# Gated linear attention and a PReLU MLP on one core: v's rows for all six levels through one copy in DRAM

## The chip, the cores and the metric

One core of a Trainium2 chip runs the whole kernel. The metric is device microseconds for one execution. The core has five engines with an instruction queue each: PE (matrix products), DVE (vector), ACT (scalar functions), POOL, and SP, which here issues all loads and stores. The data of a load or store is moved by 16 DMA engines that SP's queue feeds.

## The reference

```python
def _attn_ref(q, k, v, a_re, a_im):            # each (4, 8, 768, 48)
    mag = np.sqrt(a_re * a_re + a_im * a_im)
    scale = np.minimum(mag, 0.999) / (mag + 1e-06)
    a_re_n, a_im_n = (a_re * scale, a_im * scale)
    for t in range(S):
        ar, ai = (a_re_n[:, :, t, :, None], a_im_n[:, :, t, :, None])
        new_re = ar * S_re - ai * S_im
        new_im = ar * S_im + ai * S_re
        kv = np.einsum('bhd,bhe->bhde', k[:, :, t], v[:, :, t])
        S_re, S_im = (new_re + kv, new_im)
        y[:, :, t] = np.einsum('bhd,bhde->bhe', q[:, :, t], S_re)

def _moe_ref(x, w_in, w_out, alpha):           # x (3072, 384), d_ff 2048
    h = x @ w_in
    g = np.maximum(h, 0.0) + alpha * np.minimum(h, 0.0)
    return (g @ w_out).astype(np.float32)
```

The attention's y, with the heads of a token side by side, is the MLP's x. All is float32.

## The kernel before

**Tiling.** The sequence of each of the 4 batches is cut into 6 chunks of 128 tokens. A chunk of all 8 heads is a *unit* (24 units, u = 6 x batch + chunk). Two units make a *group* of 256 tokens, of which the MLP has 12.

**A unit.** Inside a chunk the recurrence is taken apart into six *levels*, h = 1, 2, 4, 8, 16, 32. At level h the chunk is cut into blocks of 2h tokens, and the queries of each block's second half meet the keys of its first half. DVE turns keys and queries by the phases (L579, L581) and multiplies them by decays step by step (L637, six times a unit). PE makes the products of each level (`ps_lv`, L596), DVE or ACT mask them into the tiles A, and PE multiplies A with the values of the blocks' first halves and adds all up in `ps_y` (L760). The state carried from chunk to chunk enters by L746. ACT copies the result out of PSUM (L771) and SP stores it as `ysc` (L776). `xT` (L792 and L797) is the same data read back as the MLP's input.

**The tile that the change is about.** `VL` holds for each level the values v that L760 needs: of each block of 2h tokens only h, those of its first half, shifted by one token since a unit's keys run from token 1 of the chunk. It has 128 partitions, of which each half of 64 serves two pairs of heads. One row of 96 numbers (384 bytes) is one token of two heads. There is one VL buffer, so it is loaded anew for each unit after the unit before has used it.

**How VL is filled.** Two tasks do it. `half_rows` (L480) copies, once a batch and for the levels 4, 8 and 16 only, the wanted tokens of all six chunks from v to a tensor `vsc` that also lies in DRAM: six transfers of 288 KB a batch, one for each level and each half of the heads. `loads_v` (L523 to L551) then fills VL for each unit: the levels 1, 2 and 32 directly from v (L547, ten transfers a unit), the levels 4, 8 and 16 from `vsc` (L551, two transfers). Before them it loads `V` (L523, L525, L528), all tokens of the chunk, for the state.

**The other loads.** `gates` turns the gate inputs into phases and decays, in nine pieces, and sends them to DRAM (`phs` L324, `decs` L361). `loads` brings per unit `KQ` (keys and queries, L499 and L501), `PP` (phases, L507) and `T` (decays, L514). `pieces` loads the MLP's weights in 16 pieces (L419), which ACT and DVE then put together into `w_in_sb` and `w_out_sb` (L435 to L445).

**The MLP.** The first two groups go feature by feature (`ps_h` L817, then ACT L824 and DVE L826, then `ps_o` L867). The other ten go two features at a time (L839, ACT L848 and L852, DVE L854) and through a scheme of seven half products (L957). PE takes 11,728 matmul instructions in all.

**What sets the order.** Every task is a generator; each letter of the string ORDER lets one of them go on by one step, and what that step emits is queued on its engine. So ORDER fixes, for each engine, the sequence of its instructions, SP's DMA issues included: A to I are the gate pieces, J is `loads`, K `half_rows`, L `loads_v`, M `pieces`, N and O the two weight matrices, P to m the units, n `loads_x`, o the MLP. Each engine works through its own sequence in order and waits where an input is not there yet. The numbers in `yield DMA(98)` and the like are costs by which such an order was laid out; they emit nothing.

Of the kernel before, what the change touches and what calls it, by code (L numbers as in the profile page):

```python
# [9 lines left out]
F32 = mybir.dt.float32  # L10
# [9 lines left out]
P = 128  # L20
# [7 lines left out]


ORDER = (  # L30
    "ABMAAAAMJBBABAAAAAAABAAAABAAAAAAMBBBMJJJMAAAABBAAAAAAAAAAAABBBAALKKLLJBBBBBBBBBPPPAKMNNNBJJMJBBBBBKB"
    "BPBBPBBBBBOPOPPPBPBBNJLJLBJJCCJJPPPPPNPPOOOPPLMJLLLLLKKPPQQCLLPONNNNNOOPOCCPCPPPPPPOQCNQPQPQPPCNNNCQ"
    "CCPMLLQQCCQPCCPNOOOCCCCQPPMMJJJMPPPQPQQNPPPPJLLLCQQLLJJLnJJCCNCCCCNNQQQRROQQCJLLLMJCLLLCQCCCQRNOCCCC"
    "CLLLQOQRRooooNQCCooQooQRQoOQoCRCoooooOQROQRNNQoRONoooQoooooROOMDNQQooRoOOoQQQQRQROQQRLJQLLQLDLLJJnLL"
    "LMLLLJNRDRoRRoooNDDNNSSRDRRRoRDooooRRRooRDoNoooRoRSoSRSDRoDRooooDSSoODoSoDoSSRRDRRLLLJMMJRooSRRooooR"
    "NRRLLRRLJJJLDDoSooNoNoooSoooJJMSNoooooSSDoSooooooOOONSooSSoooSSSSoToTTOSSooSJLJLJSSoooooooSooDTTDONN"
    "SSoooKLLKLLLLLLLTooSTToDNSTSTooooooooDDSOTSODOSSSSSSTTDTooTODTooooooooJMDoTNNoooooTLSSDTDTJJOTooOooo"
    "KnLLJLLJJoTOOOTTTDLLLULKLJLoToooTTooToDToUUoooooUTUToTTTooKJooooDDDDDoDoTUUoooooooDDDoooooooDLLLLDUU"
    "UUVoooooooVTTUTUTTTTVDTTLEULoooUUooooooUJJooooUUoJLEUEVUUUUUUEoooooooEooooUoUVoooEoooooUVEVVUoUUVUUo"
    "VVVEoUooVEEoKKLLLLLLLLLLLoJJJVUVUUUJoooUUooVooVoWVooooooooooEEUUEoVWEoooVVooVVVoVVoooooVVoVLLLJJLWoo"  # L40
    "oVWVVWWVEEoEWEEVVEVWWWWEVEEVLnLLLKLLLLLLooLJJJJoooooooVWVWVVVJWoVLVVooWEEoXWWoooooooooVLLEJJLLLLLJLL"
    "JJoEEEEoooooooEooLLLJLoWWWoWWLEooooooooWoXWoWoXooWoooWoooWooooEEoWooooWXXWooooWWEEEEEEooooooooooWXWW"
    "XWWWWWoJXXXoooWWoooooYoXoooooEXXoooooXXoooXLWWFLLLnJJJJFXoooooooFoJLLLLLLLLLJLLooooXXooYXFoXoXoXXXoo"
    "oooooYoXoooooXooooooXooooooXXYooYFFYXXYXYJYXYooFXFZFoYooooooooXXXXYXXoooLLLLooooYoYoYFFXXXXooYYooooo"
    "oooooooooZYYYYFooooYFFFFFooYYYooYoooYoooooJJLKKLLLJJJLLLLLLLJoooYYoooYFZZYZZFFYYJFZZFFaYYooooooooooY"
    "oooYYYYYooZFYFFLLFFoooooooooYLYLYLLZZoaoooooooooooFFnoooZZJJFZZFFFFooooZooZoFooooooooooFFoooooZooooo"
    "oooZZZZZZFFFoooLLJJLLLJLLLLFaZZoooooooZoKooZooooaZZaaZoZZaaaaZoooooooZZoZZZoaaoZaZaaooaJJGZLZGZGGZab"
    "JoooooooooooooboaaGoGGLJooGooooooooooooGaGGJLLbLLJLLLLLLLaaaaoooooaaooooooooooooooLKoGGaoaooooGbbGoo"
    "oooaaoooobbbJJKKaJooabbaooooGGGbGbGGcbGGaooooooooooooaabaaaaaabbbbaLLLLnJGGJLJooooooooooooooLLJJbcoo"
    "oooooooobbbbooooooooooooooooLKLGGGLLLbbbooooobbbbGccoooooooooooooocooobocGcLLLKKGbbbGcbbbcbooccooooo"  # L50
    "ooooooobbbbbccbbcGoooooGJJcccooooooooooooooGcccdoccoooocccoocccoLbLbLLLGGdLoGoooooJLJccoooocGcLJJJJL"
    "ccoGddoJLLeecLLLLGcooooooooooooodccdcccdooooodoccccdHddLLLJJonLoooooodddLLLLLHoHddooodHoooooooooJeHH"
    "oJLLLLLLJHoooooooooooooooeddeedddddoodoodeHoeodooodoooddooHoododdooooeeoHHoddoooddddeddeHdHHoooooooo"
    "oodoooooeooeHeeooeooLJLLLddLJLLJJJLLLJoooooooooooeeoooeHeeHeeeeeooooHHffeooooooooooooooeoJeoffJLLLLL"
    "efefeffefooffoeHoHeeeeooooefeooooooooooofeeoHHHJLeeJHfHnHooooooooooooooJoooLLJLLLLHHgffofooooHHgLJLL"
    "JHoooooooooofffoLJoJLLLLHHooooofoooHffoooooooooHgHffoooooooffgoooooHHHHHfooofofggfgffgggoooogohfooff"
    "fffffggogooooooooooogooooooffffIIIogghhJJKIooooooooooooLLLLLoooooggohgggooIIgogggoooogoooooooooogoog"
    "oooIhhgJJJJIoooooooooghgghgghohooooIhhooooooooooooooooIILJLLLLLLLLhghgghgIiihhIggIIhooooooohIIoooogg"
    "ILLLnJLLJooooooooooooooohhhhhhoIIIhhihoooooooohhooooooohohIooooooihiiiooooooooooiiohhhhoILLLLioooooo"
    "oooiIIooooooooohhLLLLiJJJJJLLhhhihhhoiLLLhhJJLLiiIIooioJJLLLLLLoooooooooooooiiooiiioooiiiijIIJJLLojI"  # L60
    "ooooioiooooooooiooiooIIiiiiijjooIJLoooooooooooooooooLijjiIIIjjjojojIIIoooooooooooooooooooIIjiiiijjij"
    "jioooooiLLLiLLLLnJLLoooooooooooooJJJJJLLLLLLjjjojjoojjojjjkoooooojjoooooooooojoooooooojjjjjjjooooooo"
    "kkkooojooooooooooooojkjkjJkoooookkkkooooooooooooooojkkooojjkkoLooooooookklooooooooooLLLLLLjjLLLkkkkk"
    "kkkkLLJJLLLJJJoooookooooookokookkooookkklooklloooooooookllkkolllokkooloooooolkoooollkklkkLJLLnlllooo"
    "ooooooooooooolllloooolllooolllooolooooooooooooooJJJoolooLLLmmLLLLLLLLLlomoomooooooloollllooooooooooo"
    "mlollmlllmLlllLLLLLLLLlmmooLLLLLmooooooooooomoooommooommmooooooooooooooooommmmmommomommooooomoooooom"
    "omoomooommmmmmmmmmmmmnoooooooooooooooooooooooooooooooooooooooooooooooooooooooooooooooooooooooooooooo"
    "oooooooooooooooooooooooooooooooooooooooooooooooooooooooooooooooooooooooooooooooooooooooooooooooooooo"
    "oooooooooooooooooooooooooooooooooooooooooooooooooooooooooooooooooooooooooooooooooooooooooooooooo")


class Ring:
# [25 lines left out]
def kernel(  # L98
# [32 lines left out]
    nc = tc.nc  # L131
# [6 lines left out]
    D2 = 2 * D  # L138
    HC = P // 2
# [6 lines left out]
    LEVELS = [h for visit in VISITS for h in visit]  # L146
# [5 lines left out]
    work = ctx.enter_context(tc.tile_pool(name="work", bufs=2))  # L152
# [33 lines left out]
    for h in (16, 32):  # L186
        by_row[h] = []
        for m in range(HC // h):
            t = next(column)
# [327 lines left out]
    def loads_v():  # L517
        for u in range(NU):
            b, c = divmod(u, NCH)
            yield DMA(172, ("KQ", u), takes=(R["V"],))  # L520
            L = loaded[u]
            L["V"] = V = work.tile([P, HP, D2], F32, tag="V", name="V", bufs=1)
            nc.sync.dma_start(V[0:P - 16], v[b, :, 1:P - 15, c].rearrange("n p e -> p n e"))  # L523
            t_ = yield DMA(24)
            nc.sync.dma_start(V[P - 16:P - 1], v[b, :, P - 15:P, c].rearrange("n p e -> p n e"))  # L525
            if c + 1 < NCH:
                t_ = yield DMA(2)
                nc.sync.dma_start(V[P - 1:P], v[b, :, 0:1, c + 1].rearrange("n p e -> p n e"))  # L528
            done["values", u] = t_
            yield DMA(98)  # L530
            VL = work.tile([P, len(LEVELS), 2, D2], F32, tag="VL", name="VL", bufs=1)
            first = True
            for k, h in enumerate(LEVELS):
                for i in range(2):
                    tokens = v[b, 2 * i:2 * i + 2, :, c].rearrange("n t e -> t n e")
                    to = VL[HC * i:HC * (i + 1), k]
                    if h <= 2:
                        runs = [(to[j::h], tokens[j + 1::2 * h]) for j in range(h)]
                    elif h == 32:
                        runs = [(to[h * m:h * (m + 1)], tokens[2 * h * m + 1:2 * h * m + h + 1]) for m in range(2)]  # L540
                    else:
                        runs = []
                    for dst, src in runs:
                        if not first:
                            yield DMA(98 // len(runs))
                        first = False
                        nc.sync.dma_start(dst, src)  # L547
            k = LEVELS.index(SPREAD[0])
            for i in range(2):
                t = yield DMA(49 * len(SPREAD), ("halves", u))  # L550
                nc.sync.dma_start(VL[HC * i:HC * (i + 1), k:k + len(SPREAD)].rearrange("p l n e -> p (l n) e"),  # L551
                                  vsc_of[u][i].rearrange("l n t e -> t (l n) e"))
# [351 lines left out]
    for m, f, c, n in blocks:  # L904
        if m < FIRST:
            i = place[m, f, c][0]
# [236 lines left out]
```

## Time and profile before

| what | us |
|---|---|
| median of three runs (766.57 to 769.87) | 768.29 |
| the profiled execution | 770.17 |
| its span, first to last instruction | 768.1 |
| PE busy | 676.6 |
| DVE busy | 605.7 |
| ACT busy | 489.4 |
| POOL busy | 12.3 |

The span is the core's own; the 2.1 us more of the profiled execution lie around it. The granted clock of PE was 0.993 on average. DMA moved 130.61 MB, at 170 GB/s on average; SP issued 700 transfers, of which 288 fill VL (240 directly from v, 48 from `vsc`) and 24 write `vsc`. In the page's slices a digit is the busy share of one fortieth of the span in tenths. In the table of stages each engine has its busy time and count of instructions in a stretch, and the last three numbers are the granted clock, the busy share of the DMA engines and the GB/s that they moved. In the rows in order of time the first two numbers are start and length in us, and brackets give the idle time of the engine just before, with what ended it.

### The profile page before, as it was taken

Reading aid. Unit: us, or ns where it says so; the run is one execution under the profiler, and the core shown is the slowest. Engines: PE = TensorE matmul, PEld = TensorE weight load, DVE = VectorE, ACT = ScalarE, POOL = GpSimd, SP = SyncE. Lnnn points to the kernel's source line nnn. Section 1 sums busy time; section 2 is a strip of 40 time slices with the busy share of each in tenths; the row PEclk is TensorE's granted clock in tenths of the full one; section 3 lists DMA queues with packets and bytes.
Section 4 is the critical chain, followed back from the end, with each engine's and each line's share of the span. In section 5 each row is a group of like instructions: output and inputs, shape, how many; then the busy total and the mean of one; then the engine's idle time right before and its main releaser. Section 6 shows DMA issues by size and latency. Waiting matters only on the chain.

```text
span 768.1 us, 26799 instructions
## 1 busy us (share of the span) xinstructions
PE 676.6 (88%) x11728; PEld 582.0 (76%) x11728; DVE 605.7 (79%) x798; ACT 489.4 (64%) x886; POOL 12.3 (2%) x48
## 2 busy tenths in 40 slices
PE   0025578999999999999999999999999999999998
PEld 0014455667767888888888888888989888989987
DVE  7889988998889899899988898878986676742323
ACT  7878986794569576858674766856776454443330
POOL 5000000000000000000000000000000000000000
PEclk9999989999999999999999999999999999999999
DMA  9999997987867775685677765683746644421000
GB/s 228 273 275 258 240 265 223 224 236 221 209 174 190 197 175 154 182 233 147 185 210 201 209 148 126 190 251 76 179 125 180 159 92 99 127 44 53 1 21 20
DMA packets 177180, 130.61 MB, mean 170 GB/s; under 512 B 66280, under 2 KB 168424, under 8 KB 176616
## 3 DMA queue, kind: packets, MB, share of 16 engines
q1 hardware_dynamic: 177064, 128.91, 63.5%
q8 instruction: 92, 1.51, 0.9%
q14 instruction: 24, 0.20, 0.1%
HBM read 100.52 MB, written 35.42 MB: 177 GB/s over the span
## 4 chain that ended last, share of the span: by engine, by line
PE 53%; DMA 17%; ACT 11%; DVE 10%; SPq 4%; issue 4%; DVEq 0%; ACTq 0%; POOL 0%; POOLq 0%
PE ps_h L839 19%; PE ps_o L957 16%; DMA T<-decs 4%; PE ps_lv L596 4%; PE ps_y L760 3%; DMA shared<-in_w_in_dram 3%; DVE KQ L637 2%; PE ps_h L817 2%; PE ps_kv L720 2%; PE ps_o L867 2%; PE ps_y L746 2%; SPq L547 1%; DMA VL<-in_v_dram 1%; DMA VL<-vsc 1%; PE ps_kt L708 1%
## 5 line engine op out<-in xcount | busy, mean ns | idle before, releaser
L839 PE MATMUL ps_h<-xT,w_in_sb 128*128 128x256 f32 x960 | 229.5, 384 | 0.8 <-DVE shared L854 0.8
L839 PEld LDWEIGHTS ps_h<-xT,w_in_sb 128*128 128x128 f32 x960 | 176.7, 190 | 22.5 <-DVE shared L854 1.6
L637 DVE TENSOR_TENSOR KQ<-KQ,T 96x1024 f32<-96x1024 f32 x120 | 145.9, 1217 | 25.3 <-PE ps_lv L596 17.6
L854 DVE TENSOR_TENSOR shared<-shared,ps_h 128x512 f32<-128x512 f32 x80 | 54.5, 682 | 73.8 <-ACT shared L852 73.6
L957 PE MATMUL ps_o<-w_out_sb,shared 128*128 128x192 f32 x624 | 111.9, 330 | 0.7 <-ACT top L973 0.4
L957 PEld LDWEIGHTS ps_o<-w_out_sb,shared 128*128 128x128 f32 x624 | 102.0, 190 | 3.4 <-ACT top L973 0.7
L848 ACT ACTIVATE shared<-ps_h 128x512 f32<-128x512 f32 x80 | 47.7, 596 | 87.5 <-PE ps_h L839 86.9
L957 PE MATMUL ps_o<-shared 128*128 128x192 f32 x448 | 81.1, 331 | 0.0
L852 ACT ACTIVATE shared<-shared,al 128x256 f32<-128x256 f32 x160 | 74.6, 503 | 1.9
L957 PEld LDWEIGHTS ps_o<-shared 128*128 128x128 f32 x448 | 73.0, 190 | 2.2 <-DVE top L984 0.2
L660 ACT COPY WQ<-KQ 96x1024 f32<-96x1024 f32 x48 | 50.0, 1041 | 38.5 <-DVE KQ L637 38.2
L596 PE MATMUL ps_lv<-WQ 96*32 96x32 f32 x2304 | 35.1, 203 | 39.9 <-DVE WQ L579 28.8
L596 PEld LDWEIGHTS ps_lv<-WQ 96*32 96x32 f32 x2304 | 26.7, 116 | 55.1 <-DVE WQ L579 27.3
L817 PE MATMUL ps_h<-xT,w_in_sb 128*128 128x256 f32 (+1 forms) x240 | 55.1, 363 | 5.2 <-DMA xT<-ysc 5.2
L867 PE MATMUL ps_o<-w_out_sb,shared 128*128 128x384 f32 x128 | 51.9, 517 | 6.0 <-DVE shared L826 4.9
L817 PEld LDWEIGHTS ps_h<-xT,w_in_sb 128*128 128x128 f32 x240 | 43.5, 208 | 17.4 <-DMA xT<-ysc 5.3
L676 ACT COPY W<-KQ 96x512 f32<-96x512 f32 x48 | 30.7, 640 | 38.9 <-DVE KQ L637 38.3
L760 PE MATMUL ps_y<-A,VL 64*48 64x64 f32 x2304 | 46.5, 224 | 3.6 <-DMA VL<-vsc 3.6
L610 ACT ACTIVATE A<-ps_lv,columns 128x64 f32<-128x64 f32 x144 | 38.6, 332 | 16.0 <-PE ps_lv L596 16.0
L760 PEld LDWEIGHTS ps_y<-A,VL 64*48 64x48 f32 x2304 | 38.4, 123 | 9.0 <-DMA VL<-vsc 4.5
L771 ACT COPY T<-ps_y 48x512 f32<-48x512 f32 x48 | 27.7, 577 | 20.2 <-PE ps_y L760 19.6
L708 PE MATMUL ps_kt<-ident,KQ 96*128 96x96 f32 x192 | 26.2, 262 | 10.3 <-DVE KQ L637 5.9
(108 smaller groups left out, 953.6 us busy)
## 6 DMA issues: line engine op xcount, KB each, us to landing
T<-decs SPq DMA_DIRECT2D x48, 384.0 KB
PP<-phs SPq DMA_DIRECT2D x24, 387.0 KB
KQ<-in_q_dram SPq DMA_DIRECT2D x48, 192.0 KB
phs<-gate SPq DMA_DIRECT2D x14, 577.5 KB
decs<-gate SPq DMA_DIRECT2D x7, 1152.0 KB
KQ<-in_k_dram SPq DMA_DIRECT2D x40, 192.0 KB
vsc<-in_v_dram SPq DMA_DIRECT2D x24, 288.0 KB
VL<-vsc SPq DMA_DIRECT2D x48, 144.0 KB
```

The lines of the kernel that those rows point to most:

```text
L596: nc.tensor.matmul(t[64 * i + j:64 * i + j + HC // 2, p], lhsT=keys(n, g), rhs=queries(n, g), start=True, stop=True)
L610: nc.scalar.activation(a[:, :, cols], t[:, :, at:at + name], AF.Copy, scale=s)
L637: nc.vector.tensor_tensor(out=x, in0=x if x0 is None else x0, in1=m, op=ALU.mult)
L660: nc.scalar.copy(z.rearrange("p i n t -> p i (n t)").rearrange("p i (m h) -> p m i h", h=h), bass.AP(tensor=KQ.tensor, offset=KQ.offset + ...
L760: nc.tensor.matmul(o, lhsT=Vp[h][64 * i:64 * i + 64, s, e_ * D:(e_ + 1) * D], rhs=a, start=False, stop=(s == 1 and h == LEVELS[-1]))
L817: nc.tensor.matmul(p, lhsT=w_in_sb[:, f // 2, kk, f % 2 * P:(f % 2 + 1) * P], rhs=x_of[m][:, kk, c * P:(c + n) * P], start=(kk == 0), stop ...
L839: nc.tensor.matmul(p[:, i], lhsT=w_in_sb[:, f // 2, kk, i * P:(i + 1) * P], rhs=x_of[m][:, kk], start=(kk == 0), stop=(kk == NK - 1))
L848: nc.scalar.activation(gt, p, AF.Relu, scale=-1.0)
L852: nc.scalar.activation(some_, some_, AF.Copy, scale=al_1[:, f + i:f + i + 1])
L854: nc.vector.tensor_tensor(out=gt, in0=gt, in1=p, op=ALU.add)
L867: nc.tensor.matmul(sums[0], lhsT=gt, rhs=w_out_sb[:, f], start=(f == start), stop=(f == stop))
L957: nc.tensor.matmul(z, lhsT=a[:, i], rhs=w[:, i], start=i == 0, stop=i == F2 - 1)
```

## The change

`SPREAD`, the list of levels that `half_rows` copies, becomes all six. The copies are twelve a batch instead of six. `loads_v` loses its direct loads; its two transfers a unit read all six levels from `vsc`, 288 KB each instead of 144. The VL tile is taken with the first of them. ORDER is a new string: 240 letters L fewer and 24 letters K more, the rest the same in number, in another sequence from the beginning on. The engines' instructions other than SP's are the same in number and form. Lines behind the edit move up, by 2 before L533 and by 19 behind it; this text names lines as the kernel before has them.

```diff
 ORDER = (
-    "ABMAAAAMJBBABAAAAAAABAAAABAAAAAAMBBBMJJJMAAAABBAAAAAAAAAAAABBBAALKKLLJBBBBBBBBBPPPAKMNNNBJJMJBBBBBKB"
+    "ABABMMAAABABAAAAAAAABMAAAAAAAAABMMMABBBANAKMABBANNAJJANABBNBBBBAAAAAAABAAABKJJJBBBBPPAKMPJJJNNNONBBB"
...
-    SPREAD = [4, 8, 16]
+    SPREAD = LEVELS
     vsc_of = {}
...
             done["values", u] = t_
-            yield DMA(98)
-            VL = work.tile([P, len(LEVELS), 2, D2], F32, tag="VL", name="VL", bufs=1)
-            first = True
-            for k, h in enumerate(LEVELS):
-                for i in range(2):
-                    tokens = v[b, 2 * i:2 * i + 2, :, c].rearrange("n t e -> t n e")
-                    to = VL[HC * i:HC * (i + 1), k]
-                    if h <= 2:
-                        runs = [(to[j::h], tokens[j + 1::2 * h]) for j in range(h)]
-                    elif h == 32:
-                        runs = [(to[h * m:h * (m + 1)], tokens[2 * h * m + 1:2 * h * m + h + 1]) for m in range(2)]
-                    else:
-                        runs = []
-                    for dst, src in runs:
-                        if not first:
-                            yield DMA(98 // len(runs))
-                        first = False
-                        nc.sync.dma_start(dst, src)
-            k = LEVELS.index(SPREAD[0])
             for i in range(2):
-                t = yield DMA(49 * len(SPREAD), ("halves", u))
-                nc.sync.dma_start(VL[HC * i:HC * (i + 1), k:k + len(SPREAD)].rearrange("p l n e -> p (l n) e"),
+                t = yield DMA(98 * 3, ("halves", u))
+                if not i:
+                    VL = work.tile([P, len(LEVELS), 2, D2], F32, tag="VL", name="VL", bufs=1)
+                nc.sync.dma_start(VL[HC * i:HC * (i + 1)].rearrange("p l n e -> p (l n) e"),
                                   vsc_of[u][i].rearrange("l n t e -> t (l n) e"))
             del vsc_of[u]
```

More of the change, by code (lines that the diff above doesn't have):

```diff
@@ L30 @@
 ORDER = (
-    "ABMAAAAMJBBABAAAAAAABAAAABAAAAAAMBBBMJJJMAAAABBAAAAAAAAAAAABBBAALKKLLJBBBBBBBBBPPPAKMNNNBJJMJBBBBBKB"
[L32 to L65, printed above, removed]
@@ L66 @@
-    "mlollmlllmLlllLLLLLLLLlmmooLLLLLmooooooooooomoooommooommmooooooooooooooooommmmmommomommooooomoooooom"
-    "omoomooommmmmmmmmmmmmnoooooooooooooooooooooooooooooooooooooooooooooooooooooooooooooooooooooooooooooo"
+    "ABABMMAAABABAAAAAAAABMAAAAAAAAABMMMABBBANAKMABBANNAJJANABBNBBBBAAAAAAABAAABKJJJBBBBPPAKMPJJJNNNONBBB"
+    "BBBBBPBBBBBBBBBBBPPPPNPOPPOPOPPPOPPOPJJLLJCJJJCLPCQQCPPPCCONNPCQCCCQQNKKKKKKKKKPPPPCPPQMJLLQCCCQQOOC"
+    "CQPCPCQPQQPCOCPQOPCCOOOCNPPPPPPPPQQQQQJJJJROCPMMPPPCMLMnJJQNLCCCLoCCCOQOOQQORCCOQQQONCCCQoooooooQCCC"
@@ new lines @@
+    "CoNNRLCJLJooDJJJRoooQRQRQQNNoRRRNoQQNRooooooQRoooooQRRQQQQQONNROoNORRQQooooQoQDDDROSooRoLLMLoRoRRRRR"
+    "DDRoJJRRRSDDooooRoDoRoDDnDoRRSooooNRRooSNNoDooooNRSJLLSRRRMJSNSoSSoODRoJJMOOOSMooooooooSoRSRRRRoRJoo"
+    "LooSoJLLJDoSSNoooooSoooooDDSSooSSSSoTMLJJJLOSSNNTNOSSooooooooooSNTooSOSOToooooTSTDNOSDoNTSooooDNSNMT"
+    "TooTSDNooJJSSSSSSSTooSoDoooTKTooDOOOoLKSSKKLoooooOoDDTOoTTToooooDLKnJKJoOooooJLJDDDTTToTToTTTToooUoT"
+    "oUoUTooLJJJooToDToUDoDTUTUUTUoDoooooDDDDDDDDDUoUTTooTooooTUTTTTUUUVTTUTToooooooUoUooooVVLEJJoLoooUUU"
@@ new lines @@
+    "UoUUUUULLEEVoooooooEoVUoooooEEEEooooUooooVoUoUVVUVUUVVVoooooEooooooEVEEEoUVUKJJJVUUUUKKKKJUVVVULLUEV"
+    "UJJJLoooooEoKoooVVVVoVooooEooEVWoVEVoWVooooVoooEoVoooooVVoWWoVWVWnEEWVVWEEWWVJLLJJJoJVWEEEoooooooooV"
+    "VVWVWVVVVVKLEJEJJoWooLJLEWJEWWXooooooLLooooooXoooooooEWWWWEJoWWWoJoooooooWoWooEoEEoEooooWooWooWooooo"
+    "WoooWoWEWEEEXEooXoYYWWoooooWWWWXWXXWoWWoooooXXXooooooooooXooooXXXXXXoWKWFoooooooooooXXXXKnooXXooXJJX"
+    "YoooooLLLLKJLFoXoooooXoXoYooXXYYXFXFYXXYYYooooooXFFYFoooooooooooXXXXYXYXXooooooXYFYoYooYFooooooooooo"
@@ new lines @@
+    "ooXLYYoooFYFYYoYooYFFooooooooooooYYFYooXLLJJJKJJJZZJKLLJJJKJKYFZooFFoooooYYooooooZooooooZZYZZYYZFZYF"
+    "YFFooooZooYYYYZYYZYYFFYYooooFooooooJJFooooooooZaZoFooaoooooooooaFFFZZFJnJoJJooooooooooFLLLLLoooFaooZ"
+    "aZZoFoZZZooZFFFFooooooZZZoooFFFFooooooFZoooooooooZooooJZoaZZaZaZZZooaoaoooooooaZZZZaZaaGLGLLoZoooZZG"
+    "aaooooooooGaoooooGooaaabbLZbKoGoooooooooaaaaaaaoooJJGbGooaooaoaooooooooaabGoooooooaGGooooooboGGaabab"
+    "aaaabGbbbbGaKKJJJKGLaJJaJooooooooooooLoJnooooGbbobboobobcoocoooooooooJoLJJJoooooobbbGobbobbboGGcoooo"
@@ new lines @@
+    "bGbooobGoooooooooooboooobcoooooGccboGccbbcooGboLLJoboooooooobboocGGGGoGGooooooocoobbbbccbbbbLJJJLccc"
+    "oooooooooocdoooooccoGGGGcocccoccocdooooooooooGooccoococLdLLJJJoodccGGcGGcccdcdcGJHooddddoooooooooooo"
+    "ooooooooooooooooodcccddoeccdoccHdHdooooooodoooeJJJHoooooddooododddHLLLHdHJLJJodeLooooodoooddoooooood"
+    "edeeddedHeooeeoooooooooooodddeodedddedeHeeeHHnooooooooooooooooooeeddddoooooooooeeeeLJJLJKeoeHeoooooo"
+    "ooKJLJJJKooooefeHoooooeoofHHfHHooooooooooooHHooofeoooffefeHfooffeHefooooooooooooeooefeJLLeeeeeeHHooo"
@@ new lines @@
+    "oooooHHooeeLLLLJKJLHJJJnoooooooooofHHHggfHoofooooffoooooooooooogJJoooooHHHHHooogfofgfffofoHHfffooooo"
+    "ooffHooooooofoooofgffgfHHggHfgofogHfooooooooooffggfffggfofggooooooooooooooooofooooooooooogghhgggoooo"
+    "ooooooogggfKKLhJJIhggogoIJLKJKJoooooooohhoooogghhggghIooohhoooooooooooohIhooooooooIIoooJJooooooooLKL"
+    "hgggghggggKggLJJIhoInLooooooooIioIoIoiJKLJJKoooooooohooIIIIooooooooohhoooooooooooioooooooooioohhihhh"
+    "hIIoooooohhoohoooooooohhooooooohhIoohioihihiiohooooIIoooooooohJLLihJhihihhhioiIIohhhhoooooIoooiIiooo"
@@ new lines @@
+    "ooooooooooiioooijiiIiioJJLJJLLJoioiiiLjjjooooLIIIIooooooooojoooooiioIIooooooooojijijijiijiooIooooooo"
+    "joiijijiijiiojojoIIjIIIiiIIILJJLooLnooooooooILJJoooooooooooooooojjjLJJJjjjjjkooooooooooookojoooojooo"
+    "ojooooooooojoooooojoojjjkjjjoooookooooooooooojkjkjkokkkooooooookoooooojkjkoookjkkjkooooooookkkkokook"
+    "kkkoooooooookoJJlookokookjLjLLLLJJJJJJkkklkloooooooooooooookkloklklkllllooooooooloooooooklklkkLoooll"
+    "lloLkkJnJJLoLLooooooooooooooollolmmolloollllooooooolooolooooolololmloolomolllmmlmoooooooooooooooooom"
@@ L68 @@
+    "mommoooooooooooooooollmmlloommloomooooooooooooooomoloommmmmmmmmoooooooomooooooomommolLLLLommmmmmmmmo"
+    "oommoooooooooooolooooooommoonooooooooooooooooooooooooooooooooooooooooooooooooooooooooooooooooooooooo"
     "oooooooooooooooooooooooooooooooooooooooooooooooooooooooooooooooooooooooooooooooooooooooooooooooooooo"
-    "oooooooooooooooooooooooooooooooooooooooooooooooooooooooooooooooooooooooooooooooooooooooooooooooo")
+    "oooooooooooooooooooooooooooooooooooooooooooooooooooooooooooooooooooooooooooooooo")
```

## The prediction

> **What bounds the kernel now.** I read first the page (busy shares and slices), then the table of stages, then the waits of PE, then SP's queue in order of time, and last DVE's line around the moments when a unit's decays arrive.
>
> ```profile
> PE 676.6 (88%) x11728; PEld 582.0 (76%) x11728; DVE 605.7 (79%) x798; ACT 489.4 (64%) x886; POOL 12.3 (2%) x48
> PE   0025578999999999999999999999999999999998
> DMA  9999997987867775685677765683746644421000
> q1 hardware_dynamic: 177064, 128.91, 63.5%
> ...
> 0.00:80.00 80.00, 17.12 (x584) 13.93 (x584) 65.99 (x101) 65.92 (x91) 10.49 (x32) 1.00 0.94 252
> 80.00:160.00 80.00, 61.99 (x1278) 47.99 (x1279) 72.13 (x99) 65.82 (x115) 0.52 (x2) 0.94 0.90 244
> 160.00:740.00 580.00, 573.40 (x9732) 497.43 (x9731) 458.74 (x585) 354.36 (x676) 1.31 (x14) 1.00 0.60 156
> ```
>
> PE is busy 676.6 of 768.1 us, so 91.4 us are idle. The stages say where: 62.9 us before 80 us, 18.0 from 80 to 160, 6.6 in the 580 us from 160 to 740, 3.9 in the tail. The first 160 us are not PE's: DVE is busy 138 us of them, ACT 132, and the DMA engines are 94% and 90% busy. From 160 us on PE has work in store and runs at 98.9%, while DMA falls to 60%. So a change in DMA traffic can reach the time in two ways: by moving the moment at which PE fills (near 160 us), and by adding to or taking from the 6.6 us of later gaps.
>
> ```profile
> 76.65 2.46 SPq L547 DMA_DIRECT2D VL<-in_v_dram  x2
> 79.22 1.28 SPq L514 DMA_DIRECT2D T<-decs  x2
> ...
> 90.18 2.62 SPq L547 DMA_DIRECT2D VL<-in_v_dram  x4
> 92.85 1.28 SPq L551 DMA_DIRECT2D VL<-vsc  x2
> ...
> 85.24 1.22 DVE L637 TENSOR_TENSOR KQ<-WQ,T 96x1024 f32<-96x1024 f32 x1 [0.44 <-DVE gate L342]
> ...
> 116.06 1.22 DVE L637 TENSOR_TENSOR KQ<-WQ,T 96x1024 f32<-96x1024 f32 x1 [0.45 <-DMA T<-decs]
> ...
> PE ps_y L760 <- DMA VL<-vsc: 3.6, 4, 1.3
> ...
> SPq L776 <- ACT T L771: 15.1, 6, 5.4
> ...
> L547 SPq DMA_DIRECT2D VL<-in_v_dram x240: 311/604/1628, 32.5 to 679.0; - x120
> ```
>
> The SP lines show that one issue holds SP's queue about 0.62 us (1.28 us for two), and that ten direct loads of VL stand in the queue for each unit. The DVE lines are the first step of units 2 and 3 that needs the decays T. T of unit 2 was issued at 79.22 and used at 85.24, just when DVE was free for it; unit 3's step at 116.06 waited 0.45 us for T. These two steps set when units 2 and 3, and with them PE's store of work, are ready. PE's own waits for VL are 3.6 us in all (columns: us in total, times, longest). The last two rows are SP's waits for ACT's copies of y in the first 180 us, and all direct loads of VL with their shortest, median and longest time in SP's queue in ns.
>
> **The change part by part.** *Issues.* Removed: 24 x 10 direct loads (L547). Added: 4 x 6 copies (L480). SP goes from 700 to 484 issues; at the median 0.604 us of the direct loads this frees 216 x 0.604 = 130 us of SP's queue. SP is in nobody's way after 160 us, where DMA is 60% busy and PE rarely waits. Between unit 0's result leaving (SP's 64th issue in the old program, 72.4 us) and unit 3's T (110.4 us), the old order has 41 issues, the new one 28 (from the 60th): 13 x 0.62 = 8 us less for SP. But the DMA engines were nearly full then: laying every transfer on SP's order at the mean time of its packets (from the trace's packet records, divided by 16 engines), I get 65.3 us of DMA work up to unit 0's result and 99.8 up to unit 3's T. That is 34.5 us of work in 38 us, so SP can give back at most 3.5 us there. I take half, 1.75; ends 0 and 3.5.
>
> *Bytes into SBUF.* The direct loads and the loads from the copy move the same 384-byte rows (29 ns each, mean), 1,536 a unit, before and after. Two transfers of 768 rows instead of twelve: nothing saved in DMA time, nothing lost.
>
> *Copies.* 24 more DRAM-to-DRAM transfers of 288 KB. The nearest rows are the copies of h=4: 32 packets of 9,216 bytes, 0.49 us each on average, so 32 x 0.49 / 16 = 0.98 us of all engines. All 24: 23.6 us spread over 768 us. After 160 us this lies beside a DMA share of 0.60 and is hidden; if that cover were gone it would delay what follows by 5.9 us a batch. The six of batch 0 fall where DMA is full: 6 x 0.98 = 5.9 us. Some other loads move too, so I count what stands ahead of the two T loads in the new order: unit 2's goes from 71.4 to 79.7 us of DMA work (+8.3: the copies, and it now stands behind one more weight piece), unit 3's from 99.8 to 105.1 (+5.3). What is queued behind these steps: DVE is in order, so the remaining steps of the unit, the MLP's L826 and the gates of the next half batch wait too, and PE's L596 waits for them.
>
> *DVE's cover.* The order moves work on DVE as well. Adding up DVE's instructions at their durations (the sum, 650 us, overlaps to 605.7 busy, so times 0.93), unit 2's step has 71.9 us of work ahead of it before and 77.2 after (+5.3); unit 3's 100.3 and 102.2 (+1.9). This work is moved, not added; while it runs DVE does not miss T. So unit 2 waits 8.3 - 5.3 = 3.0 us longer, and unit 3 5.3 - 1.9 - 1.75 = 1.7 us longer, less than unit 2 has already lost. I put the start at +3.0. Ends: -3.5 (SP's gain reaches PE whole, T is not late) and +8.3 (DVE's moved work covers nothing).
>
> *First result.* Unit 0's y now needs all twelve copies: DMA work up to its last VL load goes from 55.0 to 60.9. That load was waited for at 66.5 us, so y0 and PE's first MLP matmuls come about 6 us later than their 87.2 us. This costs nothing as long as unit 3 fills PE: the MLP work PE has between its first features and the group that needs unit 3's y is 58 us in both orders, and there were 81 us for it. If that cover were gone it costs the 6 us.
>
> *Weights.* The 16 pieces were issued by the time 133.7 us of DMA work had been queued, now 135.1. ACT's conversions of the last piece stand 7 us earlier in ACT's work. I put this at nothing.
>
> *PE's order.* The same 5,960 matmuls in another order. Taking for each pair of neighbouring lines the median gap between starts (an L839 after an L839 216 ns, an L596 after it 309, back 126), the sum over all neighbours falls by 1.8 us, mostly from 20 instead of 29 changes from L839 to L596. Taken whole, for PE is full where these stand: -1.8, ends -1.8 and 0. The distance on PE from a group's last y to its first MLP matmul is 13, 23, 65 and 123 us before and 11, 24, 67 and 129 after for groups 1 to 4: nobody starves later. So I leave the 6.6 us of middle gaps and the tail as they are; ends 0 and twice that, since a new order has new gaps.
>
> *Sum.* The profiled run took 770.17 us (768.1 span, 2.1 around it); +3.0 - 1.8 = +1.2 gives 771.4 for such a run. It lies 1.9 us above the median of the three runs, so against 768.29 the forecast is **769.5 us**: no change that counts. I call 0.5% (3.8 us, 764.4 to 772.1) what a measurement can't tell from no change.
>
> **The rivals.** *Few engines for the large copies (slower).* The h=16 copies are eight rows of 36,864 bytes. In the packet records eight such packets start between 56.15 and 56.47 us and last 1.7 us each (mean of 64: 1.72): one packet on each of eight engines, nothing on the rest. An h=32 copy has only four rows, of 73,728 bytes. If a row stays on one engine, that is two such packets one behind the other on four engines, 3.4 us a copy, and everything behind it waits for its share on those four. Batch 0 then adds 4 x 0.98 + 2 x 3.44 = 10.8 us there, not 5.9; unit 2's T comes 8.3 + 4.9 = 13.2 us later, less 5.3 of cover is +7.9, less 1.8 gives +6.1: 774.4 us. Against it: at eight engines (1.72 us a copy) the excess is 1.5 us and the whole stays at 771, inside the bound; it decides from about 2.3 us a copy, where 3.0 + 2 x (2.3 - 0.98) - 1.8 passes 3.8. The Trainium skill ("DMA: Bandwidth & Descriptors", "Why a DMA increments its semaphore by 16 and not by 1") speaks for it: a transfer uses the largest number of engines, up to 16, that divides the slowest dimension, the lowest-numbered ones, which would be 8 and 4 here. The trace agrees for the 8; no run here shows the 4 yet.
>
> *New gaps in the middle (slower).* The order was laid out with costs that differ from the chip's. Should the new one fit worse, so that the 6.6 us of gaps from 160 to 740 double, it is 1.2 + 6.6 = +7.8: 776.1 us. For it: every wait there is a local one (20-us stages lose between 0 and 1.2 us) and all places change. Against it: the stores of PE work above are equal.
>
> *SP was the brake (faster).* SP also stands 15.1 us in the first 180 us for ACT's copies of y (L776), with the loads queued behind. With fewer issues behind each such stop the loads run ahead, T is not late, and the 3.5 us are gained; PE's 1.8 us of waits for VL after 160 us go as well: -3.5 - 1.8 - 1.8 = -7.1: 761.2 us. Against it: the DMA share of 0.94 and 0.90.
>
> *It doesn't do what it says.* Excluded: the program has 48 loads and 48 copies where 288 and 24 stood.
>
> **How the numbers follow.** Forecast 0.36 (its own range 765 to 773), few engines 0.22, new gaps 0.15, SP 0.27. Faster than 764.4 is SP's case: 0.27; slower than 772.1 the two slower ones: 0.37; between 0.36. The range for 8 in 10 reaches from SP's 761 to just past the new gaps: 761 to 778.
>
> **What would show it.** Right: unit 2's first L637 with T near 93 us, after a wait for T of some 3 us; unit 3's near 120; PE's first L817 3 to 6 us later than 87.2; PE idle near 84 us up to 160 us (80.9 before) and near 7 from there to 740; PE's busy sum near 675. Few engines: packets of 36,864 bytes in pairs, four at a time, and T or PP landing late behind them. SP: T of unit 3 issued before 107 us. Wrong altogether: PE idle after 160 us above 10 us, or a fill of PE that moves by more than 5 us.

## The result, and the profile after

| | us, median (runs) | ratio to before, 95% interval |
|---|---|---|
| before | 766.57 (5, 765.19 to 769.87) | 1 |
| after | 775.23 (5, 772.37 to 777.64) | 1.0101 [1.0063, 1.0139] |
| after, on another occasion | 774.83 (8) | 1.0073 [1.0047, 1.0099] |

The change makes the kernel slower by 0.7 to 1.0%. The forecast was 769.5 us, so the median is 5.7 us above it. It was made from the 768.29 us of three runs of before; as a change it was +1.2 us, and the two ratios make it +7.7 and +5.6 us. The profiled run of after took 772.37 us with a span of 770.3; it was the fastest of its five, and the forecast for a profiled run had been 771.4. Line numbers below are those of the kernel whose rows are shown; against the kernel before, after's are lower by 2 up to L533 and by 19 behind it.

The page of after: span, busy times, the slices, and the main DMA queue (packets, MB, share).

```profile
span 770.3 us, 26539 instructions
...
PE 675.4 (88%) x11728; PEld 584.3 (76%) x11728; DVE 606.9 (79%) x798; ACT 486.0 (63%) x885; POOL 12.4 (2%) x48
...
PE   0024488889999989999999999999999999999998
...
PEclk9999687999999999999999999999999999999999
DMA  9997999889968978697479757886744945421000
...
q1 hardware_dynamic: 175112, 135.97, 68.4%
```

PE's work is the same or a little less (676.6 to 675.4), so what was lost is idle time. (ACT has one instruction fewer, a table load: 19 for 20.) In the PE slices the loss is between the fourth and the ninth digit, 58 to 173 us: 557899 before, 448888 now. The DMA queue is busy for 5 points more of the span.

The table of stages of after (PE, PEld, DVE, ACT and POOL busy, granted clock, DMA share, GB/s).

```profile
0.00:80.00 80.00, 15.52 (x552) 13.04 (x552) 66.23 (x101) 62.12 (x87) 10.82 (x32) 1.00 0.91 258
80.00:160.00 80.00, 60.11 (x1190) 46.93 (x1191) 67.66 (x95) 61.48 (x107) 0.11 (x1) 0.79 1.00 246
160.00:740.00 580.00, 573.49 (x9837) 499.53 (x9837) 463.50 (x589) 357.78 (x683) 1.44 (x15) 1.00 0.65 167
```

PE's idle time up to 160 us is 84.4 us (80.9 before), from there to 740 it is 6.5 (6.6 before). So in this execution the loss is all in the start. DVE has less busy time there than before (133.9 for 138.1 us): it waits more. Where, its rows in order of time show.

```profile
85.09 1.22 DVE L562 TENSOR_TENSOR KQ<-KQ,PP 96x1024 f32<-96x1024 f32 x1
89.78 1.36 DVE L346 SCALAR_TENSOR_TENSOR gate<-gate 128x1152 f32<-128x1152 f32 x1 [3.47 <-ACT gate L344]
...
94.36 1.22 DVE L618 TENSOR_TENSOR KQ<-WQ,T 96x1024 f32<-96x1024 f32 x1
...
121.01 1.22 DVE L618 TENSOR_TENSOR KQ<-WQ,T 96x1024 f32<-96x1024 f32 x1 [0.48 <-DMA T<-decs]
```

ACT's row for the gate step's input in after:

```profile
88.58 1.16 ACT L344 ACTIVATE gate<-gate 128x1152 f32<-128x1152 f32 x1
```

and DVE's row for the same gate step in before:

```profile
88.12 1.35 DVE L348 SCALAR_TENSOR_TENSOR gate<-gate 128x1152 f32<-128x1152 f32 x1
```

Unit 2's first step with T (L618, L637 before) starts at 94.36 us, 9.1 us later than before and 1.4 from the forecast's 93. But no bracket stands beside it: T was there. The 3.47 us were waited 4.6 us ahead of it, at the gate step L346 (L348 before), for ACT's L344. Before, this gate step stood behind unit 2's T step, at 88.12 us; the new order puts it ahead, so DVE, which works in order, reaches it before ACT has made its input. ACT's rows just before L344 show no wait for DMA, so this is a wait of the order. The rest of the 9.1 us is mainly DVE work that now stands ahead of the T step, above all the 4.6 us from L346 on.

The first MLP matmul of group 0 (L798, L817 before) starts at 89.45 us, 2.2 us later than before and not some 6 us.

SP's waits up to 80 us in after show the copies at work all the same (us in total, times, longest):

```profile
SPq L359 <- DVE gate L356: 9.2, 2, 6.0
SPq L532 <- DMA vsc<-in_v_dram: 7.7, 2, 5.7
```

Unit 0's VL load holds SP's queue until the copies have landed, and its second part is issued at 67.7 us (61.2 before). The two h=32 copies, the last of batch 0, go as four chains of packets. In the packet records the last sixteen of 36,864 bytes (eight a copy) start at 60.37, 60.51, 61.45 and 61.62 us and then three times more, 1.364 us apart in each chain; the last ends at 67.07 us. So one of these copies is two rounds of four packets, 2.73 us. All 128 packets of that size in the kernel take 1.42 us on average.

### The profile page after: what moved, and what is told of

Same layout as the page of the kernel before. It is cut to its first block, busy times and chain, and to the rows that moved or that the text cites. A ratio compares the mean times of both kernels' runs of the same rounds, so it can differ in the third digit from the quotient of the medians.

```text
span 770.3 us, 26539 instructions
## 1 busy us (share of the span) xinstructions
PE 675.4 (88%) x11728; PEld 584.3 (76%) x11728; DVE 606.9 (79%) x798; ACT 486.0 (63%) x885; POOL 12.4 (2%) x48
## 4 chain that ended last, share of the span: by engine, by line
PE 67%; DVE 11%; ACT 10%; DMA 6%; issue 3%; SPq 2%; DVEq 0%; ACTq 0%
PE ps_h L820 23%; PE ps_o L938 20%; PE ps_lv L577 5%; PE ps_o L848 4%; PE ps_y L741 4%; DVE KQ L618 3%; PE ps_kv L701 3%; PE ps_h L798 3%; PE ps_y L727 3%; DMA PP<-phs 2%; PE ps_kt L689 2%; DMA shared<-in_w_out_dram 1%; PE ps_h L938 1%; ACT W L657 1%; ACT WQ L641 1%
## 5 line engine op out<-in xcount | busy, mean ns | idle before, releaser
L618 DVE TENSOR_TENSOR KQ<-KQ,T 96x1024 f32<-96x1024 f32 x120 | 146.0, 1217 | 25.7 <-PE ps_lv L577 20.0
L798 PE MATMUL ps_h<-xT,w_in_sb 128*128 128x256 f32 (+1 forms) x240 | 54.8, 366 | 10.3 <-DMA xT<-ysc 10.3
L798 PEld LDWEIGHTS ps_h<-xT,w_in_sb 128*128 128x128 f32 x240 | 44.4, 214 | 23.3 <-DMA xT<-ysc 10.6
L848 PE MATMUL ps_o<-w_out_sb,shared 128*128 128x384 f32 x128 | 54.6, 534 | 2.4 <-DVE shared L807 2.1
L577 PE MATMUL ps_lv<-KQ,W 96*32 96x32 f32 x1536 | 24.0, 203 | 19.1 <-ACT W L657 17.5
```

The costliest lines, as they stand in the source:

```text
L577: nc.tensor.matmul(t[64 * i + j:64 * i + j + HC // 2, p], lhsT=keys(n, g), rhs=queries(n, g), start=True, stop=True)
L618: nc.vector.tensor_tensor(out=x, in0=x if x0 is None else x0, in1=m, op=ALU.mult)
L798: nc.tensor.matmul(p, lhsT=w_in_sb[:, f // 2, kk, f % 2 * P:(f % 2 + 1) * P], rhs=x_of[m][:, kk, c * P:(c + n) * P], start=(kk == 0), stop ...
L848: nc.tensor.matmul(sums[0], lhsT=gt, rhs=w_out_sb[:, f], start=(f == start), stop=(f == stop))
```

## The experiments

Each ratio is to the kernel before on the same occasion, and need not equal the quotient of the two medians. One profile scatters: the program of experiment 11 equals before up to 180 us, and its PE idles 77.8 us up to 160 where before's idles 80.9. So the ratios decide, and a profile only says where to look.

**1. The change in the old order.** Before's ORDER without the letters of the direct loads, each K twice.

```diff
-    "ABABMMAAABABAAAAAAAABMAAAAAAAAABMMMABBBANAKMABBANNAJJANABBNBBBBAAAAAAABAAABKJJJBBBBPPAKMPJJJNNNONBBB"
+    "ABMAAAAMJBBABAAAAAAABAAAABAAAAAAMBBBMJJJMAAAABBAAAAAAAAAAAABBBAALKKKKLLJBBBBBBBBBPPPAKKMNNNBJJMJBBBB"
...
```

> The change under the old order: the string of before without the letters of the ten direct loads, each copy letter doubled. Copies theory (the DMA work of batch 0's six more copies, and the four engines that an h=32 copy uses, make T and the first y late): the loss stays, 1.006 to 1.02 of before, with PE idle 3 us or more above 80.9 us up to 160 us. Order theory (the newly laid sequence fits the chip worse): 0.996 to 1.003, since the old sequence is kept.

Measured: 780.67 us, ratio 1.0132 [1.0104, 1.0161]. The change costs more in an order that was not laid out for it. The sign named for the copies in the start did not come: PE idles 82.7 us up to 160, 1.8 more than before and not 3.

**2. The new order alone.** Before's code in the new order; the ten direct loads of a unit are put back in two bursts: five where the new order has the first load from `vsc`, five and both those loads where it has the second. One place of the string, against the change's:

```diff
-    "...SSSSoTMLJJJLOSSNNT..."
+    "...SSSSoTMLLLLLJJJLLLLLLLOSSNNT..."
```

> The kernel before under the new order: three copied levels, the direct loads put back, five of them before each of the two loads from the copy. Copies theory: the loss goes, 0.997 to 1.004, T of units 2 and 3 no later than before. Order theory: 1.007 to 1.013, the loss stays without a single added copy.

Measured: 803.27 us, 1.0423 [1.0387, 1.0460], outside both cases. This says little of the order: a burst of direct loads holds SP's queue in front of what the order had planned to come next. PE idles 21.5 us between 240 and 740 us, 5.0 before. Experiment 4 asks the same without the bursts.

**3. Wide copies.** The change, but each row of an h=16 or h=32 copy is cut into 16 parts, so that no copy is of eight or four large rows.

```diff
...
+                    if P // h >= 16:
...
+                    else:
+                        w = h * one // 16
+                        src = bass.AP(tensor=rows.tensor, offset=rows.offset + one, ap=[[w, 16], [2 * h * one, P // h], [1, w]])
+                        to = to.rearrange("r (k w) -> k r w", k=16)
...
```

> The changed kernel with each copy of h=16 and h=32 cut into 16 parts a row, so that no large packet is left. Few-engines theory: the h=32 copies no longer run 5.5 us one behind the other on four engines; first y 2 to 3 us earlier than the 77.8 us of the changed kernel, ratio 1.003 to 1.007. Even-spread theory (only the bytes count): as the changed kernel, 1.008 to 1.012. Order theory: 1.008 to 1.012 too.

Measured: 773.42 us, 1.0055 [1.0027, 1.0083]. Against 1.0073 and 1.0101 for the change uncut this is 0.2 to 0.5% better, but the intervals overlap. The first y did not come earlier: in this profile it is copied out at 79.8 us, against 77.8.

**4. The new order without the added copies.** The 24 letters K for them are taken out of ORDER too. Each load of VL then reads the twelve rows that are there, so the levels 1, 2 and 32 get values that are not theirs: the kernel leaves these copies out and does not compute the reference.

```diff
-    SPREAD = LEVELS
+    SPREAD = [4, 8, 16]
...
-                                  vsc_of[u][i].rearrange("l n t e -> t (l n) e"))
+                                  vsc_of[u].rearrange("s l n t e -> t (s l n) e"))
```

> The changed kernel and its order, but only the three old levels are copied, and each load of VL reads the twelve rows that these copies make: the same transfers into SBUF, no added copies; levels 1, 2 and 32 get other values than theirs. Copies theory: 0.993 to 1.002, T of unit 2 used before 90 us (94.4 in the changed kernel). Order theory: 1.006 to 1.012. If it falls below 0.995, the freed issues of SP were worth something.

Measured: 772.28 us, 1.0027 [1.0000, 1.0053]. DVE's rows of this kernel:

```profile
89.43 1.36 DVE L346 SCALAR_TENSOR_TENSOR gate<-gate 128x1152 f32<-128x1152 f32 x1 [3.46 <-ACT gate L344]
...
94.00 1.22 DVE L618 TENSOR_TENSOR KQ<-WQ,T 96x1024 f32<-96x1024 f32 x1
```

The ratio lies between the two cases. The stop at L346 is there at the same size, and unit 2's step at the same moment within 0.4 us, with no copy added. PE idles 85.9 us up to 160 us, as in the second profile of after. Unit 0's y comes at 77.5 us too (77.8 in after), though its VL load was issued 6.1 us earlier. The start is thus late by the order. Other profiles agree: in the new order, with added copies or without, PE idles 84.4 to 86.7 us up to 160 (after twice, experiments 3 and 4), in the old one 77.6 to 82.7 (before, experiments 1, 5, 6, 7, 9 and 11). Copies make up the rest of the change's cost: 0.5 to 0.7% in ratio, some 3.5 to 5.7 us. This kernel's interval lies below that of after's first occasion and overlaps a little with that of its second, and the profiles don't show where the cost is: that of this kernel was its slowest run, that of after its fastest.

**5. The old order without direct loads and without added copies.** Experiment 4's edit in the order of experiment 1 (K once); the levels 1, 2 and 32 get values that are not theirs here too.

```diff
-    SPREAD = LEVELS
+    SPREAD = [4, 8, 16]
...
-    "...LKKKKLLJ..."
+    "...LKKLLJ..."
```

> The old order without the ten direct loads a unit and without added copies (levels 1, 2 and 32 get other values): only what SP's freed issues are worth. SP theory (SP was a brake): 0.985 to 0.994. Forecast's view (SP is in nobody's way): 0.995 to 1.000. The 1.0132 of the old order with the copies less this is what the copies cost.

Measured: 768.61 us, 1.0002 [0.9982, 1.0022]. SP loses 240 issues and the number of bytes loaded stays: worth nothing in time, though T for unit 3 leaves SP at 105.7 us (109.8 before). The added copies are what differs between this and experiment 1, with its 1.3%.

**6. Batch 0 as before, batches 1 to 3 copied**, in the old order.

```diff
+            some_levels = [4, 8, 16] if b == 0 else SPREAD
...
+            if b == 0:
...
+            else:
...
```

> The old order, batch 0 as before (three copied levels, ten direct loads a unit), batches 1 to 3 with all six levels copied. Start theory (the copies cost where the DMA engines are full, in batch 0): 0.997 to 1.003. If the copies cost in the middle too: 1.006 to 1.013, most of the loss that the old order has with all four batches copied (1.0132).

Measured: 781.67 us, 1.0159 [1.0132, 1.0186], above both cases. Taking batch 0's copies out of the full start saves nothing. The theory that the cost lies in the start fell here. SP's queue in this kernel, in order of time:

```profile
193.93 3.20 SPq L480 DMA_DIRECT2D vsc<-in_v_dram  x4
197.93 9.05 SPq L548 DMA_DIRECT2D VL<-in_v_dram  x9
207.02 1.26 SPq L552 DMA_DIRECT2D VL<-vsc  x2
```

the nine direct loads at the same place in before:

```profile
194.27 7.33 SPq L547 DMA_DIRECT2D VL<-in_v_dram  x9
```

and PE of experiment 6 soon after:

```profile
210.79 0.84 PE L768 MATMUL ps_y<-A,VL 64*48 64x64 f32 x8 [3.16 <-DMA VL<-vsc]
```

Four copies go in, the two h=32 copies of batch 1 and the first two of batch 2. The nine direct loads behind them then hold SP 9.05 us (7.33 before), unit 5's load from `vsc` leaves at 207.0 us (201.6 before), and PE waits 3.16 us for it. From 198.7 to 204.1 us the packet records show the h=32 copies as four chains again.

**7. Old order, wide copies.** Experiment 3's edit on experiment 1.

```diff
+                        to = to.rearrange("r (k w) -> k r w", k=16)
```

> The old order with the change, and the copies of h=16 and h=32 cut into 16 parts a row. Few-engines theory: 1.005 to 1.009 against 1.0132 uncut, PE's waits for VL (6.5 us up to 180 us uncut) down to 3 us or less. Even-spread theory: 1.011 to 1.015.

Measured: 775.28 us, 1.0091 [1.0059, 1.0123], against 1.0132 uncut. The gain has the sign and about the size of experiment 3's. PE's waits for VL up to 180 us are 1.7 us, where experiment 1 has 6.5, as was expected of few engines. Two rows of SP's queue behind batch 1's h=32 copies, in experiment 1:

```profile
202.86 3.76 SPq L499 DMA_DIRECT2D KQ<-in_k_dram  x1
...
218.73 1.25 SPq L512 DMA_DIRECT2D T<-decs  x2
```

and the same two here:

```profile
197.65 2.10 SPq L505 DMA_DIRECT2D KQ<-in_k_dram  x1
...
210.98 2.37 SPq L518 DMA_DIRECT2D T<-decs  x2
```

T for unit 7 leaves at 211.0 us instead of 218.7 (210.2 in experiment 5, without the copies), and group 2 begins 1.7 us later than in experiment 5 instead of 9.2 (the table below). So in this profile the loss up to group 2 is nearly gone once the rows are cut. Most of what is left, 4.3 of 6.0 us, comes behind group 2.

**8. Copies that nobody reads.** Before, complete, with six more copies a batch to a spare tensor.

```diff
...
                     nc.sync.dma_start(vsc[s, i].rearrange("n (m h) c e -> (n m) (h c e)", h=h), src)
+                    h = [1, 2, 32][i]
+                    src = bass.AP(tensor=rows.tensor, offset=rows.offset + one, ap=[[2 * h * one, P // h], [1, h * one]])
+                    yield DMA(150)
+                    nc.sync.dma_start(spare_copy[s, i].rearrange("n (m h) c e -> (n m) (h c e)", h=h), src)
...
```

> The kernel before in its own order, its direct loads kept, with six more copies a batch (levels 1, 2 and 32) into a tensor in DRAM that nobody reads, each right behind one of the old ones. If the cost of the added copies is what they take of the DMA engines and of SP's queue, the time rises as in the old-order run of the change (1.0132) or, since the direct loads still stand in the queue, a little more: 1.012 to 1.02. If the cost came from VL having to wait for copies that it needs, nothing waits for these and the ratio is below 1.005.

Measured: 791.38 us, 1.0254 [1.0193, 1.0315], above the higher case, whose end of 1.02 lies just inside the interval. Nothing waits for these copies, so the cost is what they do to the transfers beside and behind them. It is about twice that of experiment 1, whose units have 2 transfers for VL behind the copies in place of 12.

**9. The copies of batches 1 to 3 one at a time**, evenly spread, in the old order.

```diff
-    "...SSoooKKKKLLTooSTToDNSTSTooo"
+    "...SSoooKLLTooSTToDNSTSToooooo"
```

> The change in the old order (1.0132), but batches 1 to 3 have their twelve copies issued one at a time at even distances (about 10 us apart for batch 1, 12 to 18 us for the others), not two and more in a row ahead of T, KQ and VL. If the cost in the middle comes from copies that stand in bunches ahead of loads that are wanted soon, the ratio falls to 1.001 to 1.005, beside 1.0002 without any added copy. If it comes from the traffic as such (24 x 0.98 us of all DMA engines), it stays at 1.010 or more.

Measured: 780.24 us, 1.0150 [1.0090, 1.0210]: spreading helps nothing. SP's queue of this kernel:

```profile
196.21 1.38 SPq L478 DMA_DIRECT2D vsc<-in_v_dram  x2
197.69 2.15 SPq L532 DMA_DIRECT2D VL<-vsc  x2
200.14 7.41 SPq L499 DMA_DIRECT2D KQ<-in_k_dram  x1
...
217.87 2.26 SPq L512 DMA_DIRECT2D T<-decs  x2
```

and of experiment 5, the same order without added copies:

```profile
190.52 1.30 SPq L478 DMA_DIRECT2D vsc<-in_v_dram  x2
192.29 1.90 SPq L532 DMA_DIRECT2D VL<-vsc  x2
194.23 2.23 SPq L499 DMA_DIRECT2D KQ<-in_k_dram  x1
...
210.18 1.28 SPq L512 DMA_DIRECT2D T<-decs  x2
```

One issue of KQ that takes 0.62 us at the median holds SP 7.41 us, with no wait for data shown beside it. The two copies at 196.21 us are batch 1's h=32 copies; their four chains run from 202.9 to 209.7 us. T for unit 7 leaves 7.7 us later, and DVE, which had no wait at that step, now waits 1.06 us for T at 225.44 us; it does the step 8.8 us later.

**10. The copies on POOL's queue**, in the old order.

```diff
-                    nc.sync.dma_start(vsc[s, i].rearrange("n (m h) c e -> (n m) (h c e)", h=h), src)
+                    nc.gpsimd.dma_start(vsc[s, i].rearrange("n (m h) c e -> (n m) (h c e)", h=h), src)
```

> The change in the old order (1.0132), with all 48 copies issued by POOL, which is 2% busy, not by SP; place and number stay, though POOL is free to issue them earlier than SP came to them. If the cost is that the copies hold SP's queue and so delay the issues behind them, it goes and the ratio is 1.000 to 1.005. If it is the time that the copies take on the 16 DMA engines, in which loads of other queues wait just as well, the ratio stays at 1.010 or more; issued earlier they may fall into the first 160 us, where DMA is full, and cost more still.

Measured: 803.19 us, 1.0441 [1.0380, 1.0502]. POOL's rows:

```profile
128.38 4.05 POOL L478 DMA_DIRECT2D vsc<-in_v_dram  x8 [0.36 <-issue]
136.03 0.64 POOL L478 DMA_DIRECT2D vsc<-in_v_dram  x1 [3.61 <-DMA vsc<-in_v_dram]
137.22 0.58 POOL L478 DMA_DIRECT2D vsc<-in_v_dram  x1 [0.54 <-DMA vsc<-in_v_dram]
```

POOL comes to its letters early and sends ten of batch 1's copies within 10 us, into the full start. Freeing SP's queue of the copies did not help, but place and queue changed together, so this run does not tell the queue's share from the engines'.

**11. Batches 0 and 1 as before, only 2 and 3 copied**, in the old order.

```diff
-            some_levels = [4, 8, 16] if b == 0 else SPREAD
+            some_levels = [4, 8, 16] if b < 2 else SPREAD
...
-            if b == 0:
+            if b < 2:
```

> The old order; batches 0 and 1 filled as before (three levels copied, ten direct loads a unit), batches 2 and 3 wholly from copies, so that added copies fall only behind 270 us, where PE had work in store in every profile. In the profiles of the old-order runs the groups come later and later up to some 240 us and hardly later behind that: by the moments of the first MLP matmuls, 9.2 of the 11.0 us were lost by group 2. If a copy costs time only while DVE's chain is the bound, the ratio is 0.999 to 1.004, and the first L839 of group 2 stands near 234 us and that of group 6 near 658 (as before). If copies cost time wherever they run, two thirds of what batches 1 to 3 cost (1.0159) remain: 1.008 to 1.012.

Measured: 770.26 us, 1.0031 [1.0007, 1.0054]. From experiment 6 to this one only batch 1 differs: with its six added copies, and its direct loads gone, 1.3% more is lost, while the twelve copies of batches 2 and 3 together cost 0.3%. (Four of these twelve, the h=1 and h=2 copies of batch 2, go out earlier than was expected of the run, near 192 and 217 us.) The first MLP matmul of six of the groups, in us, shows where. The last column is the span. The expectation's group 6, near 658 us, is group 10 here.

| kernel | group 1 | 2 | 4 | 6 | 8 | 10 | span |
|---|---|---|---|---|---|---|---|
| before | 168.5 | 233.8 | 327.1 | 440.3 | 551.3 | 657.9 | 768.1 |
| 5: old order, no copies | 166.9 | 230.5 | 323.7 | 435.7 | 550.0 | 656.4 | 766.5 |
| 1: old order, all copies | 171.5 | 239.7 | 333.9 | 446.6 | 560.9 | 667.4 | 777.6 |
| 6: batches 1 to 3 only | 167.3 | 238.5 | 333.3 | 449.6 | 563.5 | 669.9 | 780.0 |
| 7: old order, all, rows cut | 166.8 | 232.2 | 326.4 | 441.4 | 555.8 | 662.4 | 772.6 |
| 9: all, spread | 171.5 | 239.2 | 333.6 | 445.9 | 560.7 | 667.1 | 777.3 |
| 11: batches 2 and 3 only | 166.6 | 231.3 | 324.2 | 443.2 | 552.7 | 659.1 | 769.0 |
| after (new order) | 172.8 | 238.9 | 334.5 | 448.7 | 549.5 | 660.1 | 770.3 |

Against experiment 5, experiment 1 is 4.6 us late at group 1, 9.2 at group 2 and 11.0 at group 10. Experiment 11 is about level at groups 1, 2 and 4, 7.5 us late at group 6 and back to 2.7 at group 8: there is slack behind 240 us that can take such a delay back. It does not always: experiment 6 is 8.0 us late at group 2 and 13.5 at groups 8 and 10. The stage from 160 to 240 us in one row each, for before

```profile
160.00:240.00 80.00, 78.42 (x1355) 57.99 (x1354) 70.42 (x92) 49.54 (x92) 0.26 (x3) 1.00 0.76 200
```

for experiment 1

```profile
160.00:240.00 80.00, 75.82 (x1339) 55.63 (x1338) 67.33 (x89) 46.17 (x88) 0.14 (x2) 0.98 0.82 218
```

and for experiment 11:

```profile
160.00:240.00 80.00, 79.25 (x1390) 57.96 (x1379) 71.08 (x92) 49.80 (x93) 0.26 (x3) 1.00 0.81 215
```

PE is idle 4.2 us in experiment 1 and 0.8 in experiment 11 at a DMA share of 0.82 and 0.81, so the share does not decide. DVE has 67.3 and 71.1 us of work done in the stage, and T for unit 7 leaves SP at 218.7 and 211.2 us: DVE's input comes later in experiment 1, and PE has less to do after it.

**12. After, once more**, beside experiments 5 to 7.

> The changed kernel once more, beside the next three. If its 1.0101 (1.006 to 1.014) holds, 1.007 to 1.012; if its first five runs were unlucky, about 1.005, no more than the 1.0055 that it had with its large copies cut.

Measured: 774.83 us, 1.0073 [1.0047, 1.0099]. In its profile (774.40 us, 4.2 more than before's) PE idles 85.9 us up to 160, 3.5 from there to 240 and 4.3 to 740, before's 80.9, 1.6 and 5.0; its busy sum is 2.1 us less.

## Why the prediction was right or wrong

*Sum.* The range held the time. But the single case called likeliest was a change too small to count, and a slower time came: +7.7 and +5.6 us where +1.2 was said. That the time lies inside is owed to the width of the range, whose upper end was set by new gaps from 160 to 740 us, and these did not come. Two of the terms had the right size for the wrong reason, which is luck, and one that was put at nothing was not nothing.

*DVE's cover: the start.* +3.0 was forecast; PE's idle time up to 160 us rose by 3.5 and 5.0 in the two profiles of after. But the forecast said that unit 2's step waits 3.0 us longer for T behind the copies. DVE waited 3.47 us for ACT at a gate step that the new order had moved ahead of it, and experiment 4 shows the same without copies. The forecast counted how much work of DVE's own stands ahead of T (5.3 us more); it did not ask whether each moved instruction's input would be there. The second part of T was issued at 83.7 us in after, 82.3 in experiment 4 and 79.9 in before: the copies moved it by 1.4 us, not by most of 8.3.

*First result.* Unit 0's y came 6.0 us later, as forecast (77.8 for 71.8), but experiment 4 has it at 77.5 without the copies: the order again. PE's first MLP matmul came only 2.2 us later (3.1 in the second profile), below the 3 to 6 that were named as a sign. PE's wait for xT in the first 180 us rose from 5.2 to 10.3 us (9.6 in experiment 4). That it cost nothing isn't shown; it lies within the start's loss.

*Copies.* This is the step that failed: "After 160 us this lies beside a DMA share of 0.60 and is hidden". From 160 to 240 us the share was 0.76 already before, and T and KQ, on which DVE depends, arrive in SP's order behind the copies. In the old order the added copies cost 1.3%, some 10 us, most of it by group 2 (experiments 1 and 5). The price named for a lost cover, 5.9 us a batch, was too low for batch 1: from 1.0031 to 1.0159 are 9.8 us. By these profiles a good part of the early loss hangs on the few large rows of the h=16 and h=32 copies and not on the traffic alone: with the rows whole, group 2 begins 8.0 to 9.2 us later than in experiment 5 (experiments 1, 6 and 9), with the rows cut 1.7 (experiment 7). Behind 240 us hiding holds in part: experiment 11 costs 0.3%, but experiments 6 and 7 lose 5.5 and 4.3 us more there. Batch 0's copies do not simply add to this: without them group 1 begins at 167.3 us and not 171.5, but group 2 at 238.5 and 239.7 (experiments 6 and 1). What is saved in the start is lost again behind it, where batch 0's direct loads are back in the queue. In the new order the copies cost 0.5 to 0.7%; where is open.

*Few engines for the large copies.* This rival was real as a mechanism: four chains, 2.73 us a copy, above the 2.3 us from which it was to decide, below the 3.44 of its sum; 2 x (2.73 - 0.98) is 3.5 us more than evenly spread copies. The Trainium skill's rule ("DMA: Bandwidth & Descriptors", "Why a DMA increments its semaphore by 16 and not by 1"), which gives four engines for four rows, agrees with this trace. Cutting the rows gave 0.2 to 0.5% in both orders, 1.4 to 3.5 us, though each pair of intervals overlaps; in the old order it also took away most of the loss up to group 2, in the one profile that there is.

*SP was the brake.* It fell: 240 issues fewer are worth 1.0002 [0.9982, 1.0022]. T of unit 3 did leave 4.1 us earlier in experiment 5, below the 107 us that were this rival's sign, but no time came of it.

*New gaps in the middle.* The 6.6 us became 6.5 and 7.9 in the two profiles, not 13.2. The order's gaps came in the start instead: alone it costs 0.27% [0.00, 0.53], at the edge of what could be measured.

*PE's order.* -1.8 was forecast; PE's busy sum fell by 1.2 and 2.1 us. *Bytes into SBUF* and *Weights* were put at nothing, and no run contradicts it; they were not tried alone.

No version was found that beats the kernel before; experiment 5, which equals it, leaves work out.

## What to carry to other kernels

A mean DMA share over a long stage does not say that an added transfer is hidden: ask at each place what stands behind the transfer in the queue and who waits for it, and look for issues that hold the queue longer than their own 0.6 us. Look at the number of rows of a transfer, and not only at its bytes: with the copies of eight and four rows cut up, group 2 of the old order began 7.5 us earlier. When an instruction list is reordered, a moved instruction brings its own wait along; go through the inputs of each that now stands ahead of a critical step. And a term that comes out at its forecast size is not thereby explained: undo its cause alone.

## What the hardware showed unexpectedly

- Six copies of 288 KB, 4.8 us of all 16 engines by their packets in experiment 6, cost 9.8 us of time for batch 1 (the difference of two ratios). A single issue behind two copies of four rows and two VL loads held SP 7.41 us.
- The granted clock from 80 to 160 us was 0.79 in one profile of after and 0.94 in the other, and group 1 began at 172.8 and 171.6 us: 0.15 of the clock went with 1.2 us, so PE's speed was little of what the start waited for.
- Batch 0's h=32 packets of 36,864 bytes took 1.364 us each as four chains. The h=16 ones of the same size took 1.72 us on average in the kernel before, but 1.36 to 1.43 us where eight started near 339 us: the number at once does not explain the difference.
